# Performer attention and FNet mixing in one kernel: the second part's rows transposed by VectorE and a trip through DRAM instead of by TensorE

## The chip, the cores and the metric

The kernel runs on one core of a Trainium2 chip. The engines are TensorE (PE in the profile; its weight loads are PEld), VectorE (DVE), ScalarE (ACT), GpSimd (POOL) and SyncE (SP), whose queue issues most of the DMAs here. The metric is the device time of one execution in microseconds (us), as the median of several runs.

## What is computed

All inputs and outputs are float32. The shapes are: batch 8, 8 heads, 576 positions, 64 values per head (512 in all), 128 random features, and a two-layer network with 2048 hidden values.

```python
def phi(x):                                   # random features of a row
    h = einsum('bhsd,md->bhsm', x, omega) - sum(x * x) / 2
    return exp(h - max(h)) / sqrt(m)
q_p, k_p = phi(q * scale), phi(k * scale)
kv, z = einsum('bhsm,bhsd->bhmd', k_p, v), sum(k_p, axis=2)
attn = einsum(q_p, kv) / (einsum(q_p, z) + 1e-6)       # (8, 8, 576, 64)
x = attn.transpose(0, 2, 1, 3).reshape(8, 576, 512)
u = x + real(fft(fft(x, axis=1), axis=2))
un = (u - mean(u)) / sqrt(var(u) + 1e-6)               # over the 512 values of a row
out = u + maximum(un @ w_ch1, 0) @ w_ch2               # 512 -> 2048 -> 512
```

The 8 x 576 = 4608 rows of `u` are normalized each by its own mean and variance. The change concerns the way in which the normalized rows `un` come to TensorE as a matrix with the 512 values of a row along the partitions, which the product `un @ w_ch1` needs.

## The kernel before

The first part (up to about 424 us) does attention and the Fourier mixing, batch by batch. It writes the rows `u` to a DRAM tensor `us`, and it converts the weights and makes sums of them, since the second part's products are made by a scheme with seven partial products in place of eight (a Strassen-Winograd form). Four tiles of 128 rows go through the network in the plain way in this part (`plain_of`), and the first block of the second part (j = 0) has its rows normalized and transposed there too.

The second part takes the other 4096 rows as eight blocks (j = 0 to 7) of 512 rows. For each block there are:

- `block_norms(j)`: waits for four buffers of the pool `slabs` (8 KB per partition each). Two of them become `un[0]` and `un[1]`, the transposed rows of the two halves of the block (256 rows each), and two hold sums of them (`tt`). Four tiles of 128 rows go through `norm_of`: a load of the rows `u` from `us` by SP (line 948), mean and variance on VectorE (lines 975 to 977), the power -0.5 on GpSimd (line 979), subtraction and scaling on VectorE (line 981), four transposes on TensorE into one PSUM bank (line 985), and the copy from PSUM into `un` by ScalarE (line 989). Then four VectorE passes make the sums `tt` (line 1113).
- `first_of(j, fc)` for the eight column blocks fc = 0 to 7: the first product. In each, seven products of four matmuls each in the trace (line 1252; a float32 matmul appears as two instructions), with `un` or `tt` as the moving right side of 256 columns. Copies from PSUM by ScalarE (line 1266) and sums with rectification on VectorE (line 1238) write the hidden values `hid`; the last of the seven products waits for the sum called `c22`. GpSimd makes four sums of hidden values (line 1319).
- `product_of(j, i)` for i in the order 1, 2, 4, 5, 6, 7, 3: the second product. Each has seven leaves of eight matmuls in the trace (line 1432). The weights of one leaf are 256 KB, loaded from a DRAM tensor `w2l` by SP (line 1335) into one of `NWL` = 13 buffers `wl`.
- `second_of(j)`: loads of the rows `u` once more (`ur`), and the stores of the result.

The order of the instructions on each engine is fixed when the program is built. Every piece of work is a `Step` with an engine, a planned duration, events that it comes `after`, an event that it `makes`, and buffers that it takes and gives. `Listing.run` picks again and again the step that could begin first by its own clock (plus a `bias` that shifts the choice, not the planned start) and puts its instructions next on that engine. In the first part the picks are written out (`PICKS`); in the second part they come from the clock `SECOND` alone. Each engine works its instructions in that order, and so does SP with its DMAs; real waits are by semaphores. A `NONE` step puts no instruction anywhere; a `Fork` starts a further stream of steps.

In the second part the streams are `late_norms()`, `halves()`, `loads_w2()` and `weight_sums((1, 2, 3))`. The four slabs come free when the last column block of the first product of block j - 1 has been issued, so the rows of block j are loaded, normalized and transposed during the second product of block j - 1.

Of the kernel before, what the change touches and what calls it, by code (L numbers as in the profile page):

```python
# [17 lines left out]
F32 = mybir.dt.float32  # L18
# [17 lines left out]
PE, ACT, DVE, POOL, SP, NONE = "pe", "act", "dve", "pool", "sp", "none"  # L36
# [244 lines left out]
def kernel(  # L281
# [10 lines left out]
    nc = tc.nc  # L292
# [15 lines left out]
    P = 128  # L308
# [10 lines left out]
    TP = 128  # L319
    NPLAIN = 4  # L320
    TB = 512
    NWL, NSUM = 13, 3
    NTB = (B * S - NPLAIN * TP) // TB
    HF, HT, HM = NFC // 2, TB // 2, DM // 2
    D2, F2 = NDC // 2, DFF // 2
# [621 lines left out]
    def load_rows(dst, t):  # L947
        nc.sync.dma_start(dst, us[P * t : P * (t + 1), :])
# [12 lines left out]
    def events_of(tt):  # L961
        return tuple(sorted({("us", r // S) for t in tt for r in (P * t, P * t + P - 1)}))

    unTs = {}

    def norm_of(j, t, i, pool, dst):

        yield Step(SP, 0.42, 3.0, take=("u",), kb=256)
        u = pool.tile([P, DM], F32, name="u", tag="u", bufs=2)
        load_rows(u[:], t)  # L970
        st = small.tile([P, 6], F32, name="st", tag="st")
        mv = small.tile([P, 2], F32, name="mv", tag="mv")
        rstd = small.tile([P, 1], F32, name="rstd", tag="rstd")
        yield Step(DVE, 1.12 if pool is mlpp else 1.01, bias=-0.23)
        nc.vector.bn_stats(out=st[:], in_=u[:])
        nc.vector.bn_aggr(out=mv[:], in_=st[:])
        nc.vector.tensor_scalar(rstd[:], mv[:, 1:2], 1e-6, None, op0=ALU.add)  # L977
        yield Step(POOL, 1.05 if pool is mlpp else 0.85, port=True, bias=-0.18)
        nc.gpsimd.tensor_tensor(rstd[:], rstd[:], mhalf[:], op=ALU.pow)  # L979
        yield Step(DVE, 0.455, port=True)  # L980
        nc.vector.tensor_scalar(u[:], u[:], mv[:, 0:1], rstd[:], op0=ALU.subtract, op1=ALU.mult)
        yield Step(PE, 0.437, take=("bank",), give=("u",))
        b, tp = got()
        for dc in range(NDC):
            nc.tensor.transpose(  # L985
                tp[:, 128 * dc : 128 * dc + 128], u[:, 128 * dc : 128 * dc + 128], ident[:]
            )
        yield Step(ACT, 0.5, give=(b,), makes=("unT", j, i), bias=0.33)
        nc.scalar.activation(
            out=dst,  # L990
            in_=tp.rearrange("p (d t) -> p d t", d=NDC),
            func=AF.Copy,
        )

# [102 lines left out]
    def block_norms(j, pool):  # L1097
        t0 = (NPLAIN * TP + TB * j) // 128
        yield Step(NONE, take=("slab",) * 4, after=events_of(range(t0, t0 + TB // 128)) + ("converted",))
        un = unTs[j] = [slabs.tile([128, NDC, HT], F32, name="unT2", tag="slab") for _ in range(2)]  # L1100
        tt = [slabs.tile([128, 2, D2, HT], F32, name="tt", tag="slab") for _ in range(2)]
        tts[j] = tt[0][:, 0], tt[0][:, 1], tt[1][:, 0]
        for i in range(TB // 128):
            h, k = divmod(i, HT // 128)
            dst = un[h][:, :, 128 * k : 128 * k + 128]
            yield Fork(norm_of(j, t0 + i, i, pool, dst))
        yield Step(NONE, after=tuple(("unT", j, i) for i in range(TB // 128)), bias=1.54)
        ops = sums_right(
            un[0][:, 0:D2], un[1][:, 0:D2], un[0][:, D2:NDC], un[1][:, D2:NDC], *tts[j]
        )  # L1110
        for i, (o, l, r, op) in enumerate(ops):
            yield Step(DVE, 0.6, makes=("tt", j) if i == 3 else None, port=True, bias=-0.49)
            nc.vector.tensor_tensor(out=o, in0=l, in1=r, op=op)
# [89 lines left out]
    def pairs(start):  # L1203
# [24 lines left out]
    late = ctx.enter_context(tc.tile_pool(name="late", bufs=1))  # L1228
    listing.clock = SECOND
    listing.buffers = {k: [0.0] * n for k, n in dict(  # L1230
        slab=0, u=2, ht=NFC, ur=3, s=6, set=3, wl=NWL, sums=NSUM, part=4,
    ).items()}
    w1s += [late.tile([128, 3, D2, GW], F32, name=f"w1s{g}") for g in range(1, 4)]
    hid = late.tile([128, NFC, TB], F32, name="hid")
# [5 lines left out]
    def first_of(j, fc):  # L1240

        un, tt = unTs[j], tts[j]
        f, f2 = (slice(128 * c, 128 * c + 128) for c in (fc, fc + HF))
        g = 128 * fc // GW
        fg = slice(f.start - GW * g, f.stop - GW * g)
        me = ("first", j, fc)
        lo, hi = hid[:, fc], hid[:, HF + fc]
        t1, t2 = slice(0, HT), slice(HT, TB)

        def product(ps, left, right, start):  # L1250
            for dc in range(D2):
                nc.tensor.matmul(  # L1252
                    ps[:, 0:HT],
                    lhsT=left(dc),
                    rhs=right(dc),
                    start=start and dc == 0,
                    stop=(dc == D2 - 1),
                    skip_group_check=True,
                )
# [12 lines left out]

        mm = 8 * HT / 1193.0 / 2
        yield Step(PE, mm, after=(("tt", j), ("w1s", g)), take=("bank",), bias=0.37)
        xb, x = got()
        product(x, lambda d: w1[:, d, f], lambda d: un[0][:, d], True)
        yield Fork(save("p1", x))
        yield Step(PE, mm, take=("bank",))
        zb, z = got()
        product(z, lambda d: w1s[g][:, 0, d, fg], lambda d: tt[0][:, d], True)  # L1280
        yield Fork(save("p5", z))
        yield Step(PE, mm, after=((me, "p1"),))
        product(x, lambda d: w1s[g][:, 1, d, fg], lambda d: tt[1][:, d], False)
        yield Fork(save("u2", x))
        yield Step(PE, mm, after=((me, "p5"),), makes=(me, "z"))
        product(z, lambda d: w1s[g][:, 2, d, fg], lambda d: un[1][:, D2 + d], False)
        yield Fork(added("c12", lo[:, t2], z, "u2", (zb, "s"), ((me, "z"),)))
        yield Step(PE, mm, after=((me, "u2"),), makes=(me, "u3"))
        product(
            x,  # L1290
            lambda d: w1s[0][:, 3, d, fg] if g == 0 else w1[:, d, f2],
            lambda d: un[1][:, d],
            False,
        )
        yield Fork(added("c22", hi[:, t2], x, "p5", ("s",), ((me, "u3"),)))
        yield Step(PE, mm, take=("bank",), makes=(me, "y"))
        yb, y = got()
        product(y, lambda d: w1[:, D2 + d, f], lambda d: un[0][:, D2 + d], True)
        yield Fork(added("c11", lo[:, t1], y, "p1", (yb, "s"), ((me, "y"),)))
        last = ("slab",) * 4 if fc == HF - 1 else ()  # L1300
        yield Step(PE, mm, after=((me, "c22"),), give=("set",) + last)
        product(x, lambda d: w1[:, D2 + d, f2], lambda d: tt[2][:, d], False)
# [13 lines left out]
        for i, (o, l, r, op) in enumerate(ops):  # L1316
            if i:
                yield Step(POOL, 0.75, makes=("hs", j, fc) if i == 3 else None, port=True, bias=0.56)
            nc.gpsimd.tensor_tensor(out=o, in0=l, in1=r, op=op)  # L1319
# [204 lines left out]
    def halves():  # L1524
        for j in range(NTB):
            for fc in range(HF):
                yield Step(NONE, take=("set", "ht", "ht"))
                yield Fork(first_of(j, fc))
            cells = {}
            yield Fork(second_of(j, cells))  # L1530
            for i in ORDER:
                yield Step(NONE, take=("set",))
                yield Fork(product_of(j, i, cells))

    def late_norms():
        for j in range(1, NTB):
            yield from block_norms(j, late)

    listing.run([late_norms(), halves(), loads_w2(), weight_sums((1, 2, 3))])


# [28 lines left out]
```

## Time and profile before

| | |
|---|---|
| median of 3 runs | 1178.87 us (1177.96 to 1180.17) |
| span of the profiled execution, which is its own time as far as the profile has it | 1180.9 us |
| instructions | 31428 |
| TensorE clock granted | 0.999 of full speed |
| moved by DMA | 205.67 MB, 174 GB/s over the span |
| one period of the second part (609.62 to 703.90 us) | 94.28 us |
| row tile loads (256 KB), issue to landing | 3.9 us (median) |
| weight loads of the second product (256 KB), issue to landing | 3.6 us (median) |

Lines such as L1252 are lines of the kernel before. A row of instruction groups gives engine, operation, tiles written and read, shape and count, then busy time in all and mean ns of one, then the idle time of the engine just before them and what ended it. The chain that ended last follows the work back from the last instruction; each piece has its start, its length and its place. Busy times are those of instructions; the matmuls overlap one another, so the mean of one (379 ns for 256 columns) is longer than the distance between two.

### The profile page before, as it was taken

What the parts mean: (1) busy time and instruction counts of PE and PEld (TensorE: products, weight loads), DVE (VectorE), ACT (ScalarE), POOL (GpSimd) and SP (SyncE); (2) the same over time, 40 slices, a digit from 0 to 9 for tenths busy, and PEclk for the clock granted to TensorE, in tenths of its full rate; (3) what the DMA queues carried; (4) which work ended last, traced back from release to release, by engine and by line L of the source; (5) the groups of instructions that cost most, each with busy time, mean ns of one, the idle gap of its engine ahead of it and who ended that gap; (6) DMA issues with size and microseconds to landing.
All of it is one profiled execution on the core that took longest, in us unless ns stands there. A gap on an engine that the chain in (4) does not pass through costs nothing.

```text
span 1180.9 us, 31428 instructions
## 1 busy us (share of the span) xinstructions
PE 1164.9 (99%) x12549; PEld 1044.6 (88%) x12549; DVE 722.6 (61%) x1552; ACT 452.4 (38%) x1513; POOL 412.9 (35%) x489
## 2 busy tenths in 40 slices
PE   8999999999999999999999999999999999999998
PEld 7878888779787878998998998998999899899898
DVE  7989999976677642762662572473374275266255
ACT  7987888866343212222222222222222222222211
POOL 2443544455462124214314304223322421431421
PEclk9999999999999999999999999999999999999999
DMA  8855756666662260861771582384295095177155
GB/s 238 245 165 173 244 174 180 200 197 178 188 203 91 88 224 10 291 194 52 240 242 64 174 286 85 118 293 134 63 304 179 10 301 193 44 245 236 63 169 189
DMA packets 144705, 205.67 MB, mean 174 GB/s; under 512 B 49072, under 2 KB 58544, under 8 KB 144560
## 3 DMA queue, kind: packets, MB, share of 16 engines
q1 hardware_dynamic: 144064, 203.41, 53.9%
q8 instruction: 99, 1.62, 0.6%
q14 instruction: 46, 0.38, 0.1%
q10 hardware_dynamic: 496, 0.26, 0.1%
HBM read 171.90 MB, written 35.91 MB: 176 GB/s over the span
## 4 chain that ended last, share of the span: by engine, by line
PE 90%; DVE 4%; DMA 3%; ACT 1%; issue 1%; SPq 1%; DVEq 0%; ACTq 0%
PE banks L1252 33%; PE banks L1432 30%; PE banks L1045 5%; PE banks L606 4%; PE banks L1068 4%; PE banks L512 4%; PE banks L640 2%; PE banks L687 2%; DMA kq<-in_q_dram 2%; PE banks L985 2%; PE banks L849 1%; PE banks L799 1%; DVE nmx L549 1%; PE banks L809 1%; DMA kq<-in_k_dram 1%
## 5 line engine op out<-in xcount | busy, mean ns | idle before, releaser
L1238 DVE CUSTOM_DVE_ANT_0 hid<-banks,s 128x256 f32<-128x256 f32 x192 | 79.6, 423 | 255.4 <-PE banks L1252 250.5
L1432 PE MATMUL banks<-wl,sums 128*128 128x128 f32 x1792 | 217.3, 275 | 0.0
L1432 PEld LDWEIGHTS banks<-wl,sums 128*128 128x128 f32 x1792 | 208.8, 192 | 0.4
L566 ACT ACTIVATE e<-banks,nmx 128x128 f32<-128x128 f32 x576 | 164.7, 428 | 24.5 <-DVE nmx L549 24.0
L1266 ACT ACTIVATE s<-banks 128x256 f32<-128x256 f32 x192 | 73.7, 384 | 261.1 <-PE banks L1252 261.1
L1252 PE MATMUL banks<-unT,w 128*128 128x256 f32 x704 | 167.5, 379 | 0.0
L1252 PEld LDWEIGHTS banks<-unT,w 128*128 128x128 f32 x704 | 132.7, 190 | 17.9 <-issue 0.5
L1407 ACT ACTIVATE s<-banks 128x128 f32<-128x128 f32 x168 | 46.6, 278 | 242.3 <-PE banks L1432 195.7
L1252 PE MATMUL banks<-tt,w1s 128*128 128x256 f32 x512 | 126.2, 379 | 0.0
L1319 POOL TENSOR_TENSOR hs<-hid 128x256 f32<-128x256 f32 x64 | 46.4, 725 | 207.9 <-DVE hid L1238 178.9
L1252 PEld LDWEIGHTS banks<-tt,w1s 128*128 128x128 f32 x512 | 97.3, 190 | 13.2
L1412 DVE TENSOR_TENSOR part<-banks,s 128x128 f32<-128x128 f32 x168 | 48.8, 291 | 88.6 <-PE banks L1432 88.4
L549 DVE TENSOR_REDUCE nmx<-banks 128x8 f32<-128x1024 f32 (+1 forms) x96 | 89.3, 951 | 21.6 <-PE banks L606 16.8
L1432 PE MATMUL banks<-wl,hid 128*128 128x128 f32 x768 | 97.6, 275 | 0.0
L1432 PEld LDWEIGHTS banks<-wl,hid 128*128 128x128 f32 x768 | 93.5, 192 | 1.2
L1319 POOL TENSOR_TENSOR hs<-hid,hs 128x256 f32<-128x256 f32 x64 | 46.6, 728 | 119.8 <-issue 94.9
L606 PE MATMUL banks<-om,kqT 64*64 64x128 f32 (+1 forms) x2088 | 80.2, 278 | 2.2 <-ACT kv L656 0.9
L1252 PE MATMUL banks<-unT,w1s 128*128 128x256 f32 x320 | 80.7, 379 | 0.0
L606 PEld LDWEIGHTS banks<-om,kqT 64*64 64x64 f32 (+1 forms) x2088 | 65.4, 140 | 13.8 <-issue 4.4
L979 POOL TENSOR_TENSOR rstd<-rstd,mhalf 128x1 f32<-128x1 f32 x36 | 24.8, 689 | 149.6 <-DVE rstd L977 148.6
L1432 PE MATMUL banks<-wl,hs 128*128 128x128 f32 x576 | 74.9, 275 | 0.4 <-DVE part L1412 0.4
L1432 PEld LDWEIGHTS banks<-wl,hs 128*128 128x128 f32 x576 | 70.0, 192 | 0.9 <-DVE part L1412 0.6
(128 smaller groups left out, 1951.6 us busy)
## 6 DMA issues: line engine op xcount, KB each, us to landing
wl<-w2l SPq DMA_DIRECT2D x392, 256.0 KB, 3.6
raw<-in_moe_w_ch_dram SPq DMA_DIRECT2D x32, 512.0 KB, 5.0
kq<-in_k_dram SPq DMA_DIRECT2D x32, 288.0 KB, 4.4
kq<-in_q_dram SPq DMA_DIRECT2D x32, 288.0 KB, 4.8
vd<-in_v_dram SPq DMA_DIRECT2D x32, 288.0 KB, 4.9
u<-us SPq DMA_DIRECT2D x36, 256.0 KB, 3.9
ur<-us SPq DMA_DIRECT2D x36, 256.0 KB, 3.8
out_dram<-ur SPq DMA_DIRECT2D x34, 256.0 KB, 2.4
```

What stands on the lines that cost most here:

```text
L512: nc.tensor.transpose(ps[:, (j - j0) * 128 : (j - j0 + 1) * 128], src(j), ident[:])
L549: nc.vector.tensor_reduce(nmx[:, :, 0:num], pps[:, :, 0 : MF * num].rearrange("p b (c m) -> p b c m", m=MF), axis=AX.X, op=ALU.max, negate ...
L566: nc.scalar.activation(out=e[:, c + (i if num == 1 else 0), :], in_=pps[:, i, MF * c : MF * c + MF], func=AF.Exp, bias=nmx[:, i, c : c + 1],)
L606: nc.tensor.matmul(pps[cols, c, MF * m : MF * m + MF], lhsT=kqT[rows, j, cols], rhs=om2[rows, :],)
L1045: nc.tensor.matmul(hp[:, 0:TP], lhsT=w1[:, dc, 128 * fc : 128 * fc + 128], rhs=unTs[key][:, dc, :], start=(dc == 0), stop=(dc == NDC - 1),)
L1068: nc.tensor.matmul(yp[:, 0:DM], lhsT=hs[fc][:, 128 * i : 128 * i + 128], rhs=w2[:, fc, :], start=(fc == 0), stop=(fc == NFC - 1),)
L1238: nc.vector._custom_dve(TENSOR_ADD_SAT, out=o, in0=ps, in1=sb, s0=FMAX, s1=0.0)
L1252: nc.tensor.matmul(ps[:, 0:HT], lhsT=left(dc), rhs=right(dc), start=start and dc == 0, stop=(dc == D2 - 1), skip_group_check=True,)
L1266: nc.scalar.activation(out=s[:], in_=ps[:, 0:HT], func=AF.Copy)
L1319: nc.gpsimd.tensor_tensor(out=o, in0=l, in1=r, op=op)
L1412: nc.vector.tensor_tensor(out=part[:, t, 128 * m : 128 * m + 128], in0=ps[:, 0:128], in1=saved[with_][:], op=ALU.add,)
L1432: nc.tensor.matmul(ps[:, 0:128], lhsT=left[:, f], rhs=wls[j, i, n][:, f], start=start and f == 0, stop=(f == 3), skip_group_check=True,)
```

## The change

For blocks j = 1 to 7 the four transposes on TensorE and the copy by ScalarE are replaced. After the scaling, VectorE transposes each 32 x 32 block of the tile by itself (`nc.vector.transpose` into `turn`), SP stores the result to a DRAM tensor `turned`, and four DMAs per half of a block fetch it from there into `un`, each for 32 of the 128 partitions. To make whole rows of blocks come together, the row tile is loaded in another order: tile k of a half takes every second group of 32 rows of its 256.

The slab `un` now has its columns in groups of 32: `[128, 8, 4, 32]` (groups, parts of the 512 values, rows) where it was `[128, 4, 256]`, and `tt` likewise. So the right side of a matmul of the first product consists of eight runs of 32 values, 128 values apart for `un` and 64 apart for `tt`; before it was one run of 256. This holds for block 0 too, whose rows still come by TensorE and ScalarE.

The row loads, statistics, scalings and transposes of block j are a stream of their own (`late_turns`, ahead of the others), and are tied to events of the first product of block j - 1: tile 0 and 1 are loaded after its column block 0 (event `z`), tile 2 after 3, tile 3 after 4; the statistics follow column blocks 1, 3, 4 and 6, with a bias of 4.0. The fetch into `un` waits for the slabs as the row loads did before. There is one buffer `turn` (2 KB per partition), and `NWL` goes from 13 to 12.

```diff
-    NWL, NSUM = 13, 3
+    NWL, NSUM = 12, 3
...
+    Q = 32
+    turned = {}
+
+    def by_blocks(j, i, pool, u, h, k):
+        yield Step(DVE, 0.69, take=("turn",), give=("u",), makes=("turn", j, i))
+        w = pool.tile([P, 4, NDC, Q], F32, name="turn", tag="turn", bufs=1)
+        nc.vector.transpose(
+            out=w[:].rearrange("p g d q -> p d g q"),
+            in_=u[:].rearrange("p (d g q) -> p d g q", d=NDC, g=4),
+        )
+        if (j, h) not in turned:
+            turned[j, h] = dram.tile([P, 4, 2, NDC * Q], F32, name=f"turned{j}_{h}")
+        t = turned[j, h]
+        yield Step(SP, 0.55, 6.0, after=(("turn", j, i),), makes=("turned", j, i), give=("turn",), kb=165)
+        nc.sync.dma_start(t[:, :, k], w[:].rearrange("p g d q -> p g (d q)"))
+
+    def fetched(j, h, dst):
+        yield Step(
+            SP, 1.7, 3.0, after=(("turned", j, 2 * h), ("turned", j, 2 * h + 1)),
+            makes=("unT", j, h), kb=330,
+        )
+        for g in range(4):
+            nc.sync.dma_start(
+                dst[Q * g : Q * g + Q].rearrange("q (b k) d t -> q b (k d t)", k=2),
+                turned[j, h][:, g].rearrange("(b q) k n -> q b (k n)", q=Q),
+            )
+
+    def normed(j, pool):
+        t0 = (NPLAIN * TP + TB * j) // 128
+
+        def paced(i):
+            h, k = divmod(i, HT // 128)
+            yield Step(
+                NONE,
+                after=events_of(range(t0, t0 + TB // 128)) + ((("first", j - 1, (0, 0, 3, 4)[i]), "z"),),
+            )
+            yield from norm_of(
+                j, t0 + 2 * h, i, pool, None, (h, k), ((("first", j - 1, (1, 3, 4, 6)[i]), "z"),)
+            )
+
+        for i in range(TB // 128):
+            yield Fork(paced(i))
+
-    def norm_of(j, t, i, pool, dst):
+    def norm_of(j, t, i, pool, dst, block=None, after=()):
...
-        load_rows(u[:], t)
+        if block:
+            rows = us[P * t : P * (t + 2), :].rearrange("(b k q) d -> k b q d", k=2, q=Q)
+            nc.sync.dma_start(u[:], rows[block[1]])
+        else:
+            load_rows(u[:], t)
...
-        yield Step(DVE, 1.12 if pool is mlpp else 1.01, bias=-0.23)
+        yield Step(DVE, 1.12 if pool is mlpp else 1.01, after=after, bias=4.0 if after else -0.23)
...
+        if block:
+            yield from by_blocks(j, i, pool, u, *block)
+            return
         yield Step(PE, 0.437, take=("bank",), give=("u",))
...
-        un = unTs[j] = [slabs.tile([128, NDC, HT], F32, name="unT2", tag="slab") for _ in range(2)]
-        tt = [slabs.tile([128, 2, D2, HT], F32, name="tt", tag="slab") for _ in range(2)]
+        un = unTs[j] = [slabs.tile([128, HT // Q, NDC, Q], F32, name="unT2", tag="slab") for _ in range(2)]
+        tt = [slabs.tile([128, 2, HT // Q, D2, Q], F32, name="tt", tag="slab") for _ in range(2)]
...
-            dst = un[h][:, :, 128 * k : 128 * k + 128]
-            yield Fork(norm_of(j, t0 + i, i, pool, dst))
-        yield Step(NONE, after=tuple(("unT", j, i) for i in range(TB // 128)), bias=1.54)
+            if pool is mlpp:
+                dst = un[h][:, 4 * k : 4 * k + 4].rearrange("p g d q -> p d g q")
+                yield Fork(norm_of(j, t0 + i, i, pool, dst))
+            elif not k:
+                yield Fork(fetched(j, h, un[h]))
+        parts = TB // 128 if pool is mlpp else 2
+        yield Step(NONE, after=tuple(("unT", j, i) for i in range(parts)), bias=1.54)
...
-        slab=0, u=2, ht=NFC, ur=3, s=6, set=3, wl=NWL, sums=NSUM, part=4,
+        slab=0, u=2, turn=1, ht=NFC, ur=3, s=6, set=3, wl=NWL, sums=NSUM, part=4,
...
-                    ps[:, 0:HT],
+                    ps[:, 0:HT].rearrange("f (b q) -> f b q", q=Q),
...
-        product(x, lambda d: w1[:, d, f], lambda d: un[0][:, d], True)
+        product(x, lambda d: w1[:, d, f], lambda d: un[0][:, :, d], True)
...
+    def late_turns():
+        for j in range(1, NTB):
+            yield from normed(j, late)
+
-    listing.run([late_norms(), halves(), loads_w2(), weight_sums((1, 2, 3))])
+    listing.run([late_turns(), late_norms(), halves(), loads_w2(), weight_sums((1, 2, 3))])
```

More of the change, by code (lines that the diff above doesn't have):

```diff
@@ L990, in norm_of @@
             out=dst,
-            in_=tp.rearrange("p (d t) -> p d t", d=NDC),
+            in_=(
+                tp.rearrange("p (d t) -> p d t", d=NDC)
+                if len(dst.shape) == 3
+                else tp.rearrange("p (d g q) -> p d g q", d=NDC, q=Q)
+            ),
             func=AF.Copy,
@@ L1104, in block_norms @@
             h, k = divmod(i, HT // 128)
-            dst = un[h][:, :, 128 * k : 128 * k + 128]
-            yield Fork(norm_of(j, t0 + i, i, pool, dst))
-        yield Step(NONE, after=tuple(("unT", j, i) for i in range(TB // 128)), bias=1.54)
+            if pool is mlpp:
[5 more added lines that the diff above has]
+        yield Step(NONE, after=tuple(("unT", j, i) for i in range(parts)), bias=1.54)
         ops = sums_right(
-            un[0][:, 0:D2], un[1][:, 0:D2], un[0][:, D2:NDC], un[1][:, D2:NDC], *tts[j]
+            un[0][:, :, 0:D2], un[1][:, :, 0:D2], un[0][:, :, D2:NDC], un[1][:, :, D2:NDC], *tts[j]
         )
@@ L1279, in first_of @@
         zb, z = got()
-        product(z, lambda d: w1s[g][:, 0, d, fg], lambda d: tt[0][:, d], True)
+        product(z, lambda d: w1s[g][:, 0, d, fg], lambda d: tt[0][:, :, d], True)
         yield Fork(save("p5", z))
         yield Step(PE, mm, after=((me, "p1"),))
-        product(x, lambda d: w1s[g][:, 1, d, fg], lambda d: tt[1][:, d], False)
+        product(x, lambda d: w1s[g][:, 1, d, fg], lambda d: tt[1][:, :, d], False)
         yield Fork(save("u2", x))
         yield Step(PE, mm, after=((me, "p5"),), makes=(me, "z"))
-        product(z, lambda d: w1s[g][:, 2, d, fg], lambda d: un[1][:, D2 + d], False)
+        product(z, lambda d: w1s[g][:, 2, d, fg], lambda d: un[1][:, :, D2 + d], False)
         yield Fork(added("c12", lo[:, t2], z, "u2", (zb, "s"), ((me, "z"),)))
@@ L1291, in first_of @@
             lambda d: w1s[0][:, 3, d, fg] if g == 0 else w1[:, d, f2],
-            lambda d: un[1][:, d],
+            lambda d: un[1][:, :, d],
             False,
@@ L1297, in first_of @@
         yb, y = got()
-        product(y, lambda d: w1[:, D2 + d, f], lambda d: un[0][:, D2 + d], True)
+        product(y, lambda d: w1[:, D2 + d, f], lambda d: un[0][:, :, D2 + d], True)
         yield Fork(added("c11", lo[:, t1], y, "p1", (yb, "s"), ((me, "y"),)))
@@ L1301, in first_of @@
         yield Step(PE, mm, after=((me, "c22"),), give=("set",) + last)
-        product(x, lambda d: w1[:, D2 + d, f2], lambda d: tt[2][:, d], False)
+        product(x, lambda d: w1[:, D2 + d, f2], lambda d: tt[2][:, :, d], False)
         yield Step(ACT, 0.37, 0.1, give=(xb,), makes=(me, "c21"), bias=0.73)
```

## The prediction

> **What bounds the kernel now.** I read the busy shares first, then the chain that ended last over one period of the second part, then busy time by stretch, the order inside one column block, and last the groups, waits and DMA. The page's busy shares, and below them the chain (start, length, what):
>
> ```profile
> PE 1164.9 (99%) x12549; PEld 1044.6 (88%) x12549; DVE 722.6 (61%) x1552; ACT 452.4 (38%) x1513; POOL 412.9 (35%) x489
> ...
> 654.63 6.05 PE banks L1252 x28
> ...
> 662.43 15.19 PE banks L1432 x136
> 677.62 0.93 PE banks L985 x8
> 678.54 16.08 PE banks L1432 x144
> 694.63 0.04 issue
> 694.67 1.11 PE banks L985 x8
> 695.78 8.12 PE banks L1432 x72
> ```
>
> TensorE bounds the run. From 423.7 us to the end the chain is its own matmuls: L1252 is the first product, L1432 the second, L985 the transposes of the next block's rows. They stand in the chain, so one that goes shortens the run by its length unless something takes its place.
>
> Busy time in the two stretches of one period, first product and then second (window, us, busy PE, PEld, DVE, ACT, POOL, then clock, DMA share, GB/s):
>
> ```profile
> 609.62:662.43 52.81, 52.81 (x266) 46.98 (x266) 14.87 (x33) 12.35 (x35) 21.94 (x30) 1.00 0.22 73
> 662.43:703.90 41.47, 41.43 (x370) 41.12 (x369) 32.86 (x70) 9.22 (x29) 8.06 (x10) 1.00 0.90 294
> ```
>
> VectorE is busy 28% of the first stretch and 79% of the second, the DMA engines 22% and 90%. The change moves loads and statistics from the second into the first, where there is room, and puts a fetch into the second, where there is little. One column block of the first product in order of time:
>
> ```profile
> 641.69 0.42 DVE L1238 CUSTOM_DVE_ANT_0 hid<-banks,s 128x256 f32<-128x256 f32 x1 [0.44 <-PE banks L1252]
> ...
> 642.94 0.73 POOL L1319 TENSOR_TENSOR hid<-hid 128x256 f32<-128x256 f32 x1
> ...
> 645.93 0.73 POOL L1319 TENSOR_TENSOR hs<-hid,hs 128x256 f32<-128x256 f32 x1 [2.26 <-issue]
> 646.11 0.42 DVE L1238 CUSTOM_DVE_ANT_0 hid<-banks,s 128x256 f32<-128x256 f32 x1 [3.99 <-PE banks L1252]
> ...
> 646.87 0.42 DVE L1238 CUSTOM_DVE_ANT_0 hid<-banks,s 128x256 f32<-128x256 f32 x1 [0.34 <-PE banks L1252]
> ...
> 649.26 1.03 PE L1252 MATMUL banks<-tt,w 128*128 128x256 f32 x4
> ```
>
> Between the last sum of one column block (ends 642.12) and the first of the next (646.11) VectorE is free for 3.99 us; GpSimd is free from 643.67 to 645.93. The sum that starts at 646.87 ends at 647.29, and the product that must wait for it starts at 649.26: 1.97 us to spare. Now the prices of one row tile (busy us, mean ns, idle before), the weight queue's wait, and two DMA rows (KB, us to landing):
>
> ```profile
> L981 DVE TENSOR_SCALAR u<-u,mv,rstd 128x512 f32<-128x512 f32 x28 | 21.2, 778 | 3.1 <-POOL rstd L979 3.1
> L979 POOL TENSOR_TENSOR rstd<-rstd,mhalf 128x1 f32<-128x1 f32 x28 | 19.7, 702 | 130.4 <-DVE rstd L977 129.4 <-DMA wl<-w2l 1.0
> L975 DVE BATCH_NORM_STATS2 st<-u 128x6 f32<-128x512 f32 x28 | 19.1, 684 | 0.0
> L1113 DVE TENSOR_TENSOR tt<-unT,tt 128x512 f32<-128x512 f32 x14 | 9.5, 681 | 0.0
> ```
> ```profile
> SPq L1335 <- PE banks L1432: 461.0, 320, 27.2
> ```
> ```profile
> wl<-w2l SPq DMA_DIRECT2D x392, 256.0 KB, 3.6
> u<-us SPq DMA_DIRECT2D x36, 256.0 KB, 3.9
> ```
>
> **Removed: the transposes of blocks 1 to 7.** A period lasts 703.90 - 609.62 = 94.28 us. By the chain, 28 matmuls of L1252 take 6.05 (0.216 each) and 144 of L1432 take 16.08 (0.1117). A block has 8 x 7 x 4 = 224 of the first and 7 x 7 x 8 = 392 of the second: 48.3 + 43.8 = 92.1. The rest, 2.16 us, is the two groups of transposes (0.93 + 1.11) and the turns into and out of them. Seven blocks: **15.1 us off**. Block 0 and the four plain tiles keep theirs. The 28 evictions on ScalarE (0.6 us each) were beside the matmuls; they give nothing.
>
> **Added to the first stretch: statistics, scaling and VectorE's transpose.** No row has a transpose by VectorE. The nearest are 128x512 passes: from 0.54 (L981 undisturbed) to 1.50 (L981's longest, beside GpSimd). [...] Does a tile fit one gap? From 642.12 the statistics (0.68 + 0.18 + 0.15) end at 643.13; GpSimd's power starts when its third sum ends, 643.67, and ends at 644.37; the scaling takes 0.54 to 644.91, the transpose to 645.60; the next sum starts at 646.11. It fits with 0.5 us over. With a 1.50 transpose the sums start 0.3 late, within the 1.97. The cover is that margin; without it each late 0.1 us costs 28 x 0.1 = 2.8. I take 0. VectorE's second stretch loses about 6 us of its 33, which buys nothing since TensorE doesn't wait there.
>
> **Moved: the row loads.** Four issues of 0.39 us per block pass from ahead of the weight loads to the first product, where the queue sits in the wait shown (up to 27 us for the first freed weight buffer). Tile i is loaded after products 0, 0, 3, 4 and read after 1, 3, 4, 6: at least one column block (6.05 us) between, against a landing of 3.9. Late landing would hold VectorE's sums behind it. I take 0; bounds 0 and, for one landing 1 us past its gap's margin in each block, 7.
> [...]
>
> **Added: the store.** 512 packets of 512 bytes; such packets take 28 ns here (mean of the 4608 of that size in the first part), so 0.9 us of the 16 engines per tile, in a stretch with 78% free. It waits in SP's queue for the transpose; behind it are only weight loads whose buffers are taken. 0 us.
>
> **Added to the second stretch: the fetch.** Eight issues of about 0.42 (the loads' rows have 0.32 to 0.42): 3.4 us on SP, during which some four freed weight buffers wait. 1024 packets of 1 KB at 56 ns / 16 = 3.6 us of the engines, against 512 of 2 KB at 98 / 16 = 3.1 for the loads that leave: the DMA share goes from 0.90 to 0.91. With packets as slow as the 2 KB ones it is 6.3 and 0.98, still not over.
>
> **Weight buffers 13 to 12.** A buffer freed at the end of one leaf (eight matmuls, 0.893) is read again 11 leaves later, 9.8 us (before: 10.7). The row has 3.6 us from issue to landing, 6.9 at the longest. Behind the fetch: 2.5 late at the issue, then 3.6 of fetch in the rings and about 2 of its own, 8.1 of 9.8. Bounds 0 and 7 x 1.5 = 10 us (all at their worst, 11.3); I take 0.
>
> **The first product's right side read in runs of 32 floats.** No matmul in this trace reads so. Lower end 0. Upper end: two 128-column matmuls cost 0.2234 where one of 256 costs 0.2158, so 7.6 ns for a new start; seven of them in each of 1792 would be 95 us. I take 0: on VectorE a pass that reads an operand backwards (L749, 128x510) takes 685 ns like the straight ones, so a pattern as such isn't charged there.
>
> **Sums of the turned block.** Same size, L1113's 0.68, now earlier in the second stretch and waiting for the fetch. 0 us; rival 1 prices it.
>
> Sum: 1178.87 - 15.1 = 1163.8, and 0.6 for small waits at new places (0.1 a block, some turns like the chain's 0.04 issue): **1164.4 us**. The profiled execution has a span of 1180.9, 2.0 over the median; I take the saving off the median, as the periods are the same work.
>
> [...]
>
> **Rivals.**
> 1. *Slower: the fetch lands after the sums have their turn on VectorE.* VectorE's order is fixed beforehand, so the sums block the evictions behind them. By the planner's terms they come about 6.5 us after the slabs are free (2 x 1.7 + 3.0 + 0.15); by the rows the last issue ends at 3.4 and lands 3.6 to 6.9 later, so 0.5 to 3.8 late. Evictions have perhaps 0.5 to 2 to spare. It decides from 15.1 / 7 = 2.2 us of TensorE wait per block; at 3.3 the time is 1163.8 + 23 = 1187. For it: 90% DMA in that stretch. Against: VectorE itself is loaded there and will come later than planned.
> 2. *Part is given back.* If the power is queued behind GpSimd's fourth sum (ends 646.66), scaling and transpose end at 648.6, two sums more make 649.4, and the product at 649.26 waits 0.2 or more; with weights 1 us late per block as well, 28 x 0.2 + 7 = 12.6 at most: about 1170 in the middle. For it: the in-order queues; against: the 2.26 us hole.
> 3. *The runs are charged.* Even at 1.2 ns for each of 12,544 new runs the gain is gone (15.1): 1179; at a full 7.6 it is 1259. Against: no row; it would be an odd price.
> That nothing changes because transposes are hidden is excluded by the chain.
>
> **How the numbers follow.** Forecast (1163 to 1168) 0.66; rival 2 (1168 to 1176.5) 0.12; rival 1 0.13; rival 3 0.09, of which 0.03 near no change. Faster 0.77, within 0.2% 0.03, slower 0.20 (1 +- 0.2%, 1176.5 to 1181.2, is what a measurement of this kernel can tell). The range goes from 1162.8 (floor less the runs' spread of 1) to 1180, leaving some 0.2 above. The forecast's own range is 1163 to 1168.
>
> **What would show it.** Right: L985 with 32 matmuls instead of 144 in all, a period of 92.1 to 92.3, L1252 at 0.216 each, no wait of TensorE for wl or for VectorE. Wrong: L1252 longer per matmul (rival 3); VectorE idle ahead of L1113's line for the fetch, with TensorE waiting after it (1); TensorE waiting in the first product for the sum into hid, or at the start of the second for wl (2).

## The result, and the profile after

The changed kernel takes **1168.71 us** (median of 5, 1166.67 to 1174.67); the kernel before takes 1179.1 on the same chip (1177.96 to 1180.17). The ratio is 0.9917, with a 95% interval from 0.9894 to 0.9940. So it is faster, by 10.4 us; 14.5 were forecast (1178.87 to 1164.4).

First the page's busy shares and then, from the chain that ended last, one block's second product (start, length, what). In the changed kernel L1310 is the first product, L1490 the second, L988 the fetch and L1393 the weight loads.

```profile
PE 1153.5 (98%) x12437; PEld 1032.9 (88%) x12437; DVE 754.7 (64%) x1573; ACT 436.8 (37%) x1485; POOL 430.4 (37%) x496
...
707.23 36.26 PE banks L1310 x168
...
752.18 1.48 PE banks L1490 x14
753.66 5.73 DMA wl<-w2l
759.40 0.04 issue
759.44 35.10 PE banks L1490 x312
794.55 5.18 PE banks L1310 x24
```

112 matmuls are gone, the four transposes of 28 tiles, and none stands in the chain of the second part any more. But a DMA now does: a load of weights that was on its way for 5.73 us, and TensorE waited for its end at 759.4. The waits of the two TensorE rows over the second part that end at a named cause (us in total, times, longest):

```profile
PEld banks L1490 <- DMA wl<-w2l: 4.5, 7, 1.6
PEld banks L1490 <- DVE part L1470: 0.6, 1, 0.6
PEld banks L1310 <- DVE hid L1296: 0.4, 1, 0.4
```
```profile
PE banks L1490 <- DMA wl<-w2l: 3.1, 5, 1.4
```

The kernel before has no wait for `wl` on TensorE. What was issued on SP around that place, and what SP itself waited for over the second part:

```profile
751.35 0.32 SPq L1393 DMA_DIRECT2D wl<-w2l  x1
751.72 1.85 SPq L988 DMA_DIRECT2D unT<-turned  x4
753.66 0.38 SPq L1393 DMA_DIRECT2D wl<-w2l  x1
754.14 1.80 SPq L988 DMA_DIRECT2D unT<-turned  x4
756.04 38.86 SPq L1393 DMA_DIRECT2D wl<-w2l  x45
```
```profile
SPq L1393 <- DMA wl<-w2l: 9.9, 22, 1.3
SPq L1393 <- DMA unT<-turned: 9.5, 34, 0.6
```

One weight load got in between the two halves of the fetch; it is the one that landed late. The second row of the waits is new as well: SP waits for the landing of the fetch before it issues a weight load. The trace has the semaphore of each DMA's landing: the first 826 of SP's 828 issues have eight of them in turn. Behind the fetch above, the weight loads issued at 757.13, 757.82 and 759.46 us each came 0.06 us after the landing of the DMA issued eight before (757.07, 757.76 and 759.40); the first of these three landings is that of the fetch issued at 752.66. The eight DMAs of a block's fetch are as many as the semaphores.

On TensorE, around the wait:

```profile
752.02 1.95 PE L1490 MATMUL banks<-wl,hid 128*128 128x128 f32 x16
753.80 4.63 PE L1490 MATMUL banks<-wl,sums 128*128 128x128 f32 x40
759.44 1.16 PE L1490 MATMUL banks<-wl,hid 128*128 128x128 f32 x8 [1.01 <-DMA wl<-w2l]
```

The kernel's own order of loads and leaves, laid beside the trace, says which buffer is which. The buffer of the late load came free at 753.07, when the first of the two leaves at 752.02 ended, and the leaf that reads the load is the one at 759.44: only six leaves lie between the two. Where nothing waits (experiment 2) the reading comes 5.2 us after the buffer is free, and not the 9.8 us of the prediction. The leaves aren't read in the order in which their weights are loaded, because in this order the leaves of several second products alternate.

The best measure for what follows is the second part alone, from the first matmul of block 0's first product to the last one of block 7's second product, since the unchanged first part ended anywhere from 418.8 to 423.8 us in the profiles of this study. Before it took 752.68 us. Less the 15.1 of the prediction's first step it would be 737.6. TensorE's granted clock over the second part is 1.00 in every profile.

| profile | second part, us | over 737.6 | time between the last leaves of two blocks (up to block 6), us |
|---|---|---|---|
| before | 752.68 | | 94.28 to 94.30 |
| after | 743.75 | 6.2 | 92.34 to 93.85 |
| after, on a second chip | 739.56 | 2.0 | 92.17 to 92.84 |

By the prediction's count the matmuls of a block last 92.1. What lies above is waiting, and it changes from block to block and from run to run. The kernel before took the same time for each of these blocks.

In the first stretch all went well. One tile in VectorE's order, with GpSimd:

```profile
731.44 0.42 DVE L1296 CUSTOM_DVE_ANT_0 hid<-banks,s 128x256 f32<-128x256 f32 x1 [0.44 <-PE banks L1310]
731.78 0.69 DVE L1022 BATCH_NORM_STATS2 st<-u 128x6 f32<-128x512 f32 x1
...
732.95 0.55 POOL L1026 TENSOR_TENSOR rstd<-rstd,mhalf 128x1 f32<-128x1 f32 x1 [2.55 <-DVE rstd L1024]
733.47 0.72 POOL L1377 TENSOR_TENSOR hs<-hid 128x256 f32<-128x256 f32 x1
733.53 0.94 DVE L1028 TENSOR_SCALAR u<-u,mv,rstd 128x512 f32<-128x512 f32 x1 [0.67 <-POOL rstd L1026]
...
734.51 0.71 DVE L972 STREAM_TRANSPOSE turn<-u 128x512 f32<-128x512 f32 x1
...
735.86 0.42 DVE L1296 CUSTOM_DVE_ANT_0 hid<-banks,s 128x256 f32<-128x256 f32 x1 [0.64 <-PE banks L1310]
```

The whole chain fits in the gap between two column blocks, and VectorE is idle for 0.64 us before the next sum, which starts when TensorE has its operand.

### The profile page after: what moved, and what is told of

It is laid out like the page before. It is cut to its first block, busy times and chain, and to the rows that moved or that the text cites. A ratio compares the mean times of both kernels' runs of the same rounds, so it can differ in the third digit from the quotient of the medians.

```text
span 1172.2 us, 31328 instructions
## 1 busy us (share of the span) xinstructions
PE 1153.5 (98%) x12437; PEld 1032.9 (88%) x12437; DVE 754.7 (64%) x1573; ACT 436.8 (37%) x1485; POOL 430.4 (37%) x496
## 4 chain that ended last, share of the span: by engine, by line
PE 88%; DMA 5%; DVE 4%; ACT 2%; SPq 1%; issue 1%; DVEq 0%
PE banks L1310 33%; PE banks L1490 27%; PE banks L1099 5%; PE banks L606 5%; PE banks L1122 4%; PE banks L512 4%; DMA wl<-w2l 3%; PE banks L640 2%; PE banks L687 2%; PE banks L849 2%; PE banks L799 1%; ACT e L566 1%; DVE nmx L549 1%; DMA kq<-in_k_dram 1%; PE banks L809 1%; PE banks L860 1%
## 5 line engine op out<-in xcount | busy, mean ns | idle before, releaser
L1490 PE MATMUL banks<-wl,sums 128*128 128x128 f32 x1792 | 217.4, 275 | 0.0
L1490 PEld LDWEIGHTS banks<-wl,sums 128*128 128x128 f32 x1792 | 208.6, 192 | 0.0
L1310 PE MATMUL banks<-unT,w 128*128 128x256 f32 x704 | 166.3, 379 | 0.0
L1310 PEld LDWEIGHTS banks<-unT,w 128*128 128x128 f32 x704 | 133.2, 190 | 18.3 <-issue 0.5
L1530 POOL TENSOR_TENSOR ur<-ur,part 128x512 f32<-128x512 f32 x32 | 47.3, 1479 | 267.1 <-ACT part L1523 187.0
L1310 PE MATMUL banks<-tt,w1s 128*128 128x256 f32 x512 | 126.3, 379 | 0.0
L1310 PEld LDWEIGHTS banks<-tt,w1s 128*128 128x128 f32 x512 | 97.0, 190 | 13.7 <-DVE hid L1296 0.4
L1490 PE MATMUL banks<-wl,hid 128*128 128x128 f32 x768 | 100.0, 276 | 3.2 <-DMA wl<-w2l 3.1
L1490 PEld LDWEIGHTS banks<-wl,hid 128*128 128x128 f32 x768 | 94.0, 192 | 6.0 <-DMA wl<-w2l 4.5
L1310 PE MATMUL banks<-unT,w1s 128*128 128x256 f32 x320 | 79.5, 379 | 0.0
L1490 PE MATMUL banks<-wl,hs 128*128 128x128 f32 x576 | 75.1, 275 | 0.5 <-DVE part L1470 0.4
L1490 PEld LDWEIGHTS banks<-wl,hs 128*128 128x128 f32 x576 | 70.1, 192 | 1.2 <-DVE part L1470 0.6
L1377 POOL TENSOR_TENSOR hs<-hid,hs 128x256 f32<-128x256 f32 x64 | 50.1, 784 | 57.2 <-issue 37.1
L1310 PEld LDWEIGHTS banks<-unT,w1s 128*128 128x128 f32 x320 | 60.4, 190 | 8.7
```

Source lines behind the costliest of these rows:

```text
L1310: nc.tensor.matmul(ps[:, 0:HT].rearrange("f (b q) -> f b q", q=Q), lhsT=left(dc), rhs=right(dc), start=start and dc == 0, stop=(dc == D2 - 1),
L1490: nc.tensor.matmul(ps[:, 0:128], lhsT=left[:, f], rhs=wls[j, i, n][:, f], start=start and f == 0, stop=(f == 3), skip_group_check=True,)
L1530: eng.tensor_tensor(out=o, in0=o, in1=other, op=ALU.add)
```

## The experiments

Two theories were set against each other at first. By theory 1 TensorE waits for weights that the fetch holds up. By theory 2 the loss is in the first stretch, where the scaling takes longer than before.

**1. No fetch.** Blocks 1 to 7 work on the slabs that block 0 filled.

```diff
-        yield Step(
-            SP, 1.7, 3.0, after=(("turned", j, 2 * h), ("turned", j, 2 * h + 1)),
-            makes=("unT", j, h), kb=330,
-        )
-        for g in range(4):
-            nc.sync.dma_start(
-                dst[Q * g : Q * g + Q].rearrange("q (b k) d t -> q b (k d t)", k=2),
-                turned[j, h][:, g].rearrange("(b q) k n -> q b (k n)", q=Q),
-            )
+        yield Step(
+            NONE, 0.0, 6.5, after=(("turned", j, 2 * h), ("turned", j, 2 * h + 1)),
+            makes=("unT", j, h),
+        )
...
-        un = unTs[j] = [slabs.tile([128, HT // Q, NDC, Q], F32, name="unT2", tag="slab") for _ in range(2)]
-        tt = [slabs.tile([128, 2, HT // Q, D2, Q], F32, name="tt", tag="slab") for _ in range(2)]
+        if not j:
+            once.append([slabs.tile([128, HT // Q, NDC, Q], F32, name="unT2", tag="slab") for _ in range(2)])
+            once.append([slabs.tile([128, 2, HT // Q, D2, Q], F32, name="tt", tag="slab") for _ in range(2)])
+        un, tt = once
+        unTs[j] = un
```

> Left out: the fetch of the turned rows into un (blocks 1 to 7 work on the slabs of block 0; everything else, the VectorE transposes and stores too, stays). Theory 1 (TensorE waits for weights that were issued and carried behind the fetch): the waits for wl at the start of the second products go, and the time is the floor of the prediction, 1179.1 - 15.1 = 1164.0 us, with a spread between runs as small as that of the kernel before (about 2 us). Theory 2 (the loss sits in the first stretch, where the scaling on VectorE takes 0.94 instead of 0.54 us and the sums into hid come later): the time stays at 1168 to 1169.

Measured: 1166.31 us (1166.23 to 1167.35), ratio 0.9888 (0.9875 to 0.9902). There is no wait for `wl` left, and the spread is small, as theory 1 has it; but it is not quite the floor. The second part is 739.55, 2.0 over. In this run a single row load of the first block landed late:

```profile
424.11 11.17 DMA u<-us
435.28 0.02 issue
435.30 0.71 DVE st L1017
```

It is on its way for 11 us, behind the first weight loads, and holds VectorE's statistics and then a sum into `hid` for which TensorE waits (1.0 us on the weight-load row). That is a price of the moved loads, once in the run, not in each block. The planner's order also came out otherwise here (its blocks take 86.4 and 98.2 in turn). The remaining 1 us stands mostly in three gaps of 0.3 us on TensorE, for which the profile names no cause.

**2. The fetch as whole rows.** In DRAM the turned rows are laid so that each half is one DMA with 4 KB for each of 128 partitions. The store of a tile becomes four DMAs, in the first stretch.

```diff
-            turned[j, h] = dram.tile([P, 4, 2, NDC * Q], F32, name=f"turned{j}_{h}")
+            turned[j, h] = dram.tile([4, Q, 4, 2, NDC * Q], F32, name=f"turned{j}_{h}")
...
-        nc.sync.dma_start(t[:, :, k], w[:].rearrange("p g d q -> p g (d q)"))
+        for bq in range(4):
+            nc.sync.dma_start(
+                t[:, :, bq, k].rearrange("g q n -> q g n"),
+                w[:].rearrange("p g d q -> p g (d q)")[Q * bq : Q * bq + Q],
+            )
...
-        for g in range(4):
-            nc.sync.dma_start(
-                dst[Q * g : Q * g + Q].rearrange("q (b k) d t -> q b (k d t)", k=2),
-                turned[j, h][:, g].rearrange("(b q) k n -> q b (k n)", q=Q),
-            )
+        nc.sync.dma_start(
+            dst[:].rearrange("p c d t -> p (c d t)"),
+            turned[j, h].rearrange("g q b k n -> (g q) (b k n)"),
+        )
```

> The turned rows lie in DRAM so that each half is fetched by one DMA of 128 partitions with 4 KB each, in place of four DMAs of 32 partitions with packets of 1 KB; the store of a tile becomes four DMAs in the first stretch. The same bytes, the same places in the planner. Theory 1: the fetch holds SP about 0.9 us instead of 3.6 per block and the rings about 2.8 us (256 packets of 4 KB at 159 to 200 ns / 16 engines) instead of 5 to 6; the waits for wl fall from 0.2 to 1.7 us a block to nearly none: 1164.0 to 1165.5 us. Theory 2: no change, 1168 to 1169.

Measured: 1165.82 us (1164.52 to 1167.77), ratio 0.9883 (0.9869 to 0.9897). The second part is 737.67: 0.1 over the floor. Every block takes 92.12. Theory 2 falls: the first stretch is as it was, with the scaling at 0.94, and nothing is lost.

**3. The fetch later and in two places.**

```diff
             SP, 1.7, 3.0, after=(("turned", j, 2 * h), ("turned", j, 2 * h + 1))
+            + ((("second", j - 1, (2, 5)[h]), "read"),),
```

> The fetch as it is, but its two halves are tied to the last reads of the first and fourth of the seven second products (2 and 5), so some 6 and 25 us later and apart. Theory 1, if the pile-up of eight issues at one place does the harm: each half delays the weights by half as much, under their margin, 1164.5 to 1166 us. If instead the bytes in that stretch do it (DMA share near 1 in all of it): as now, 1168 to 1169, with the waits for wl at two places. Theory 2: 1168 to 1169.

Measured: 1167.02 us (1165.44 to 1168.71), ratio 0.9892 (0.9877 to 0.9907). Five of six blocks take 92.12, one takes 95.08, and TensorE's row still waits 2.2 us for `wl` in three places. The second part is 740.95. It helps most blocks and not the time as a whole: the medians can't tell it from the changed kernel. The planner's order changed with it (1594 of TensorE's 12437 instructions stand elsewhere), so the place of the fetch isn't tested alone here.

**4. Thirteen weight buffers.** The constant goes back to 13; for the memory, the turned tile takes a buffer of the first part.

```diff
-    NWL, NSUM = 12, 3
+    NWL, NSUM = 13, 3
...
-        w = pool.tile([P, 4, NDC, Q], F32, name="turn", tag="turn", bufs=1)
+        w = ur1[:].rearrange("p (g d q) -> p g d q", g=4, d=NDC)
```

> Thirteen weight buffers as before; the turned tile takes the place of a buffer of the first part that is free by then, so the memory suffices. Theory 1 with the buffer count as its other half: 0.89 us more between a buffer's release and its next reading, so waits of 0.2 to 1.7 us a block (5.4 in all in the profiled run) shrink to 0 to 0.8: 1165 to 1166.5 us. If the twelfth buffer is beside the point: 1168 to 1169. Theory 2: 1168 to 1169.

Measured: 1175.73 us (1174.43 to 1177.3), ratio 0.9963 (0.9949 to 0.9976). None of the expectations has that. The waits for `wl` are gone, and others have come, in each block alike (93.62):

```profile
PEld banks L1490 <- ACT s L1465: 5.5, 7, 0.8
PEld banks L1490 <- POOL hid L1377: 3.4, 6, 0.6
```

The planner counts the weight buffers too, and with one more it chose another order for all engines: 2130 of TensorE's 12437 instructions stand elsewhere than in the changed kernel. So this run doesn't test the buffer; experiment 7 does.

**5. The changed kernel again, and whole rows beside it.**

> The changed kernel once more, on the chip of the three others of this set, so that they are compared with it and not only with the kernel before: 1167 to 1169 us, with 1 to 6 us of TensorE's waits for wl in the second part and a spread between runs of several us.

> One DMA per half, 128 partitions, 4 KB each: second part 737.7 us as in its first run (752.7 - 15.0), no wait for wl, and a median 2 to 4 us below the changed kernel on this chip.

Measured on one chip: the changed kernel 1167.61 us (1165.68 to 1170.02), ratio 0.9897 (0.9879 to 0.9915); whole rows 1164.95 (1164.48 to 1165.41), ratio 0.9874 (0.9856 to 0.9892). Both ratios are to 1178.88, so whole rows are 2.7 us better than the change, and each of their four runs is below each of its five. The second part is 739.56 and 737.69. The chain of the latter over one second product is a single piece, to be set beside the four pieces of the changed kernel:

```profile
746.66 41.09 PE banks L1493 x368
787.76 5.18 PE banks L1313 x24
```

**6. What makes the fetch harmful: the issues, the packets or the partitions?** Both kernels have the DRAM layout of experiment 2. The first fetches by four DMAs of 32 partitions with 4 KB each, the second by four DMAs of 128 partitions with 1 KB each.

```diff
+        for g in range(4):
+            nc.sync.dma_start(
+                dst[Q * g : Q * g + Q].rearrange("q c d t -> q (c d t)"),
+                turned[j, h][g].rearrange("q b k n -> q (b k n)"),
+            )
```
```diff
+        for b in range(4):
+            nc.sync.dma_start(
+                dst[:, 2 * b : 2 * b + 2].rearrange("p c d t -> p (c d t)"),
+                turned[j, h][:, :, b].rearrange("g q k n -> (g q) (k n)"),
+            )
```

> Rows in DRAM as in the run with one DMA per half, but fetched by four DMAs of 32 partitions with 4 KB each: as many issues on SP as in the changed kernel, each on a quarter of the partitions, without the small packets. If the small packets (1 KB at 73 ns in the second part) fill the rings: the waits go, second part 737.7 to 738.5. If it is SP's 3.6 us or the narrow set of partitions: waits of 1 to 6 us stay.

> The same rows fetched by four DMAs of 128 partitions with 1 KB each: as many issues, as many and as small packets as in the changed kernel, but over all partitions. If the narrow set of partitions is what makes the fetch run at 195 GB/s: it runs at 300 or more and the waits go, 737.7 to 738.5. If the issues on SP or the packet size do it: waits of 1 to 6 us stay.

Measured: 32 partitions with 4 KB 1168.86 us (1164.8 to 1169.51), second part 739.97, with waits for `wl` as in the changed kernel (1.3 us on the weight-load row; 1.2 in the changed kernel on this chip); 128 partitions with 1 KB 1165.31 (1162.92 to 1166.34), second part 738.31, with 0.2 us of them left. From the records of the DMA packets, over the seven fetches of each run (issues: from the first to the last; rate: all bytes moved while fetch packets were under way):

```
                          issues on SP   first issue to end   rate in
                          (median)       of last packet       that time
changed kernel            3.8 us         7.4 to 9.3 us        215 to 242 GB/s
4 x 32 partitions, 4 KB   3.7            7.2 to 8.8           237 to 255
4 x 128 partitions, 1 KB  3.8            6.5 to 7.6           268 to 293
1 x 128 partitions, 4 KB  1.9            5.9 to 7.3           326 to 368
```

The rows of the changed kernel and of the last are over two profiles each. As many issues and as small packets do little harm when all partitions take part (the second part is 0.7 us over 737.6), though the rate of 268 to 293 GB/s stays under the 300 that was expected; large packets on 32 partitions at a time (237 to 255 GB/s) help hardly at all (2.4 us over, and 2.0 in the changed kernel on this chip). So the narrow set of partitions is the larger cause. In single microseconds in which over 95% of the bytes were the fetch's and the engines were counted as busy, the narrow fetches (two profiles of the changed kernel, one of 4 x 32) moved 166 to 238 GB/s (means 198 and 208 with 1 KB, 215 with 4 KB); the 2 KB weight packets behind them, where they moved alone, 387 (median).

**7. Thirteen buffers, the planner's order kept.** The planner counts 12, the memory has 13. On TensorE and GpSimd every instruction stands where it stands in the changed kernel, and SP's DMAs have the same order.

```diff
-        w = pool.tile([P, 4, NDC, Q], F32, name="turn", tag="turn", bufs=1)
+        w = ur1[:].rearrange("p (g d q) -> p g d q", g=4, d=NDC)
...
-                    wl = late.tile([128, 4, 128], F32, name="wl", tag="wl", bufs=NWL)
+                    wl = late.tile([128, 4, 128], F32, name="wl", tag="wl", bufs=NWL + 1)
```

> Thirteen weight buffers in memory, while the planner still counts twelve, so that every engine's order is that of the changed kernel; the turned tile lies in a buffer of the first part. If the thirteenth buffer is what the fetch lacks: waits for wl of 2 to 6 us in the second part fall to 0 to 1, second part 737.7 to 738.7 us. If SP, which has the weight loads in the changed kernel's order behind the fetch, or the rings are what binds, the buffer helps little: 739 to 744 as in the changed kernel's two profiles.

Measured: 1163.74 us (1162.92 to 1167.86), ratio 0.9872 (0.9853 to 0.9890). The second part is 737.49, every block 92.12, no wait for `wl`. The fetch is as slow as ever (212 to 243 GB/s, 7.8 to 9.0 us from the first issue to the end), and it no longer matters:

```profile
748.00 41.09 PE banks L1490 x368
789.10 5.18 PE banks L1310 x24
```

The loads themselves say by how much. Apart from two waits of 0.1 and 0.3 us for the 22nd, TensorE's waits for weights in the two profiles of the changed kernel are for the 15th and the 16th of a block's 49 weight loads. For these two, the us from the release of the buffer to the issue, the landing and the reading (medians of blocks 0 to 6; two numbers are two profiles):

```
                                 15th load                    16th load
                                 issued  landed    read if    issued  landed    read if
                                                   no waits                     no waits
before (13 buffers)              0.0     2.7       4.3        0.0     3.5       5.2
changed kernel                   0.6     5.4, 4.9  5.2        2.1     7.5, 7.0  7.0
4 x 128 partitions, 1 KB         0.6     4.1       5.2        2.1     6.5       7.0
1 x 128 partitions, 4 KB         0.0     4.0, 3.7  5.2        0.0     5.6, 5.0  7.0
changed, 13 buffers, 12 planned  0.0     4.4       7.0        0.6     5.6       7.9
```

The changed kernel has nothing to spare in either place. The thirteenth buffer moves the reading, and a wide fetch the landing.

**8. The layout alone, and twelve buffers alone.** The first has the runs of 32 in `un` and `tt`, but TensorE's transposes in all blocks and 13 buffers; the second is the kernel before with one constant changed.

```diff
-            if pool is mlpp:
+            if True:
...
-    listing.run([late_turns(), late_norms(), halves(), loads_w2(), weight_sums((1, 2, 3))])
+    listing.run([late_norms(), halves(), loads_w2(), weight_sums((1, 2, 3))])
```
```diff
-    NWL, NSUM = 13, 3
+    NWL, NSUM = 12, 3
```

> Of the change only the layout of un and tt in runs of 32: all blocks still have TensorE's transposes and ScalarE's copies, 13 weight buffers, nothing in the first stretch. If the runs cost nothing (as the changed kernel's 36.26 us for 168 matmuls, 0.2158 each, says): the time of the kernel before, 1178 to 1180 us, second part 752.7. If a part of the loss is in the layout: longer by 2 to 5 us.

> The kernel before with 12 weight buffers, and nothing else. The planner's order may change a little. If 9.8 us are enough for loads that land after 3.6 (6.9 at the longest): 1178 to 1181 us and no wait for wl.

Measured: the layout alone 1180.47 us (1176.76 to 1183.8), ratio 1.0004 (0.9993 to 1.0016), second part 752.65 against 752.68. The runs cost nothing. Twelve buffers alone: 1184.46 us (1182.79 to 1187.24), ratio 1.0044 (1.0028 to 1.0060), second part 757.97. TensorE doesn't wait for `wl` there either; it waits for VectorE's scaling ahead of the transposes:

```profile
PEld banks L985 <- DVE u L981: 6.2, 7, 0.9
```

As in experiment 4 the planner's order is another (1508 of TensorE's instructions stand elsewhere). That this order is the cause, and not the buffer, is argued here from the wait that is named; no run has the kernel before's order with 12 buffers.

## Why the prediction was right, and where it was not

The sign and the mechanism held. Its point, 1164.4, was 4.3 us too low, and the measured 1168.71 lies just above the forecast's own range to 1168, in rival 2; the 1167.61 of the second chip lies inside it.

- **Removed transposes, 15.1 us off.** Right to the tenth: where nothing waits (experiments 2 and 7) the second part is 15.0 and 15.2 us shorter than before.
- **Statistics, scaling and transpose in one gap.** Right as to the end, with 0.64 us to spare where 0.5 was worked out, though two terms were off and one was in the wrong order. The transpose takes 0.711 in all 28 places; the 0.69 behind the prediction's end at 645.60 is the planner's number for it, which no run shows for a transpose. The planner put GpSimd's power before its sums rather than behind the third of them, so it came sooner and took 0.55 us (0.70 taken), and the scaling runs beside the first of those sums and takes 0.94 instead of 0.54.
- **The moved loads, 0.** Right for six blocks and nearly for the first: VectorE waited 3.4 us for one load there in the changed kernel's profile, with at most the 0.4 shown above passed on to TensorE. The packets of the load issued at 717.74 us were under way from 719.33 to 723.27 (67 GB/s), so the last ended 5.5 us after the issue, where such loads took 3.9 before. The statistics started at 725.74, 8.0 us after the issue, so it cost nothing.
- **The store, 0.** Right.
- **The fetch, "3.6 us of the engines", and the weight buffers, "I take 0".** This is the step that failed, and it failed by the 9.8 us more than by the price. The delay worked out behind the fetch was 8.1 us (2.5 at the issue, 5.6 to the landing); the late load above took 6.3 (0.6 and 5.7), and the medians of the 15th and 16th loads are 4.9 to 5.4 and 7.0 to 7.5. But these loads are read 5.2 and 7.0 us after their buffers come free. "Read again 11 leaves later" took the leaves to be read in the order of the loads; for these two, six and eight leaves lie between, and before the change four and six. Against 5.2 and 7.0 the prediction's own 8.1 would have given a wait of 1 to 3 us a block. TensorE waited 0.1 to 1.7 us a block, 2.0 to 6.2 in all in two profiles; that it wasn't more is because the loads came sooner than the 8.1. The fetch itself was priced too low: its 1 KB packets took about 73 ns where 56 was taken, the mean of that size in the kernel before, and the whole of it 7.4 to 9.3 us from the first issue. The upper end given for the buffers, 10 us, held.
- **Runs of 32 floats.** Right: 36.26 us for 168 matmuls is 0.2158 each, as before, and the layout alone changes nothing. The upper end of 95 us was far too careful.
- **Sums of the turned block, and rival 1.** They don't hold anything: no TensorE wait for them shows. In the block above the first of them starts at 763.72, well after the fetch.
- **Rival 2** was what came in part: not by the power on GpSimd's queue but by "weights 1 us late per block", and "about 1170" was near. Its sign, TensorE waiting for `wl` at the start of the second product, is what the profile shows.

The loss needs both halves. A wide fetch with 12 buffers loses nothing (experiment 2), a narrow fetch with 13 buffers loses nothing (experiment 7). By the table in experiment 7, four DMAs per half make the 16th load 2.1 us late at its issue, whether they are narrow or wide, and narrow ones let it land 0.5 to 1 us later still. SP's wait for the DMA eight issues before isn't what held TensorE at 759.4: there it shows from the 17th load (issued at 757.13) on, and these loads had 1.4 us and more to spare. Whether it has a part in the 0.1 and 0.3 us of the 22nd load was not shown.

## What to carry to other kernels

Here the work taken from a full engine was worth its length in the chain, 15.0 and 15.2 us for 15.1; ask next which queue the replacement stands in, and how many microseconds the loads behind it have to spare. Take that for the tightest load, from the leaf that frees its buffer to the leaf that reads it, and not from the number of buffers: here it was 5.2 us where 9.8 had been worked out. A DMA's price is to be taken from rows with the same set of partitions, not only the same packet size: fetch to all 128 partitions at once (268 to 368 GB/s here, 212 to 255 by 32 at a time), by laying the rows out in DRAM for it where the store has time. Where a planner fixes the order, a constant such as a buffer count is two changes in one; give memory and planner their own numbers before drawing conclusions from either.

## What the runs showed of the hardware and was not expected

- DMAs to 32 partitions at a time moved 166 to 238 GB/s with the engines counted as busy, whether by packets of 1 or 4 KB; weight loads to all partitions behind them 387 (median).
- A scaling pass on VectorE takes 0.54 us alone and 0.94 in all 28 places where a GpSimd sum of 128x256 began at about the same time. In the kernel before its longest was 1.50.
- VectorE's transpose of a 128x512 float32 tile in blocks of 32x32 takes 0.711 us, the same in all 28 places, about one plain pass (0.68).
- With a weight buffer fewer and nothing else, the kernel before becomes 5 us slower, and with one more the changed kernel 7 to 8, both with another order of the planner. In the changed kernel the order is the cause: with the order kept, the thirteenth buffer makes it faster (experiment 7).
